# Four interleaved attention layers: VectorE's share of the exponentials chosen tile by tile from its estimated backlog

## The chip, the cores and the metric

The kernel runs on one core of one Trainium2 chip. Five engines work side by side, each on its own in-order queue: TensorE (PE; its weight loads are listed apart as PEld), VectorE (DVE), ScalarE (ACT), GpSimd (POOL) and SyncE (SP), which issues most DMAs. The metric is the device time of one execution in microseconds (us). The kernel before took 2195.17 us, the median of three runs (2189.13 to 2195.78).

## The reference

```
x = A_x                                   # 2048 rows x 640, bf16
x = x + A_ref(layernorm(x), A_wqkv, A_wo) # layer 0: windowed, each row sees the 256 rows up to itself
x = x + B_ref(layernorm(x), B_wqkv, B_wo) # layer 1: full attention
x = x + A_ref(layernorm(x), A_wqkv, A_wo) # layer 2: windowed
x = x + B_ref(layernorm(x), B_wqkv, B_wo) # layer 3: full attention
# each: 32 heads of width 20; q, k, v from x @ wqkv; softmax(q k / sqrt(20)) v; then @ wo
```

A full layer takes the exponential of 32 x 2048 x 2048 scores; these dominate the work.

## The kernel before, in words

Rows are cut into four chunks of 512 (`c`), heads into eight groups of four (`g`). A *unit* is one layer, chunk and head group (`class Unit`). A full unit has 16 key blocks of 128 (`kc`) times 4 heads (`j`): 64 *banks*, a bank being the 128 x 512 scores of one head, one key block and one chunk of queries, one of the eight PSUM banks. Chunk 0 of a full layer is split into parts by key blocks (`PARTS`), so that it can begin before all keys are there.

The program is written out by a planner in Python that runs over *tiles* (`t`, one tick of `state["tick"]` each). In a tile, PE writes up to three banks of scores (L1359) into PSUM banks 0 to 2 (even tiles) or 3 to 5 (odd tiles), and ACT takes their exponential in one instruction (L1387). Some tiles later PE multiplies them by the values (L1420), accumulating in bank 7 (`op`). Between these, `background` gives out work of other kinds as *tasks* (`todo`, ordered by the unit that needs them, and `tails`, which go first): normalisation and its transposes (`t_ln`, L447), projections of values (`t_v`) and of keys and queries (`t_block`), the softmax division (`t_tail`, L1128), the output projection (`t_out`, L579). Every task needs a PSUM bank from `take_m`. After the early part of the program only bank 6 is left for that (`mfree`); its contents are drained by DVE (`evac`, L331) or by the operation of the task. Where a unit needs something that has not been issued, `start_unit` calls `require`, which issues the missing tasks on the spot, ahead of the unit's first scores. `keep_clock` adds matmuls whose result nobody reads (`unread`), so that PE stays active.

Keys, queries and values of the full layers go through DRAM: `t_block` writes keys with a DMA from POOL's queue (L546), and `load_unit` loads them for a unit through SP's queue, values first (L798), then four strips of queries (L810) and keys (L812) by turns. `load_ahead` loads a unit early when everything is ready.

DVE computes some of the exponentials itself. Such banks are *set aside* (`aside`), always in pairs: PE writes the scores of each, DVE turns them into fixed point (L957), and once two are there a chain of four operations on 1024 columns follows (`t_chain`, L969, L978, L980, L982). `side_values` multiplies the result by the values (L1010). The number per unit is fixed ahead: `put_aside` gives 4 to each unit of chunks 1 to 3 of layer 1 (`SIDE_1`), and 6 or 8 by turns to the units of chunks 1 to 3 of layer 3 (`SIDE_3`); the first such unit of layer 3 gets none, the last 4. In layer 1 a set-aside bank takes the third place of a tile, so that ACT gets two banks; the list `tiles` is made in advance and spaces them five tiles apart. In layer 3 (`side["late"]`) the set-aside scores come on top of the tile's three and use bank 6 (`side_scores`, L944).

`state["lag"]` estimates how far DVE is behind, in us: each DVE operation adds its estimated time, each tile takes off the time that ACT needs for it. `side_work` issues operations of a chain while the estimate is below `WORK`; in layer 3, set-aside scores are taken while it is below `LAG`.

The order of the units: layer 0 with chunk 0 of layer 1 woven in; then chunks 1 to 3 of layer 1 with layer 2's finished chunks woven in; then chunk 0 of layer 3 (key blocks 0 to 11, with the last chunk of layer 2 woven in, then key blocks 12 to 15); then chunks 1 to 3 of layer 3.

Of the kernel before, what the change touches and what calls it, by code (L numbers as in the profile page):

```python
# [25 lines left out]
G = 8  # L26
# [13 lines left out]
LAG = 0.5  # L40
WORK = 1.0
SIDE_1 = 4
SIDE_3 = (6, 8)
# [9 lines left out]
def kernel(  # L53
# [272 lines left out]
    def evac(out_, in_):  # L326
        if state["act"]:
            nc.scalar.copy(out=out_, in_=in_)
        else:
            state["lag"] += 0.6  # L330
            nc.vector.tensor_copy(out=out_, in_=in_)  # L331
# [60 lines left out]
    def stats(l, c, i):  # L392
        if (l, c) not in mvs:
            mvs[l, c] = lnp.tile([P, 4, 2], F32, name="mv", tag="mv")
        state["lag"] += 1.2
# [287 lines left out]
    def put_aside(l, c, g):  # L683

        if l == 1:
            n = SIDE_1
        else:
            n = 4 if (c, g) == (NC - 1, G - 1) else SIDE_3[g % 2]
        if n == 2:
            return ((NT - 1, 2), (NT - 1, 3))  # L690
        return tuple((NT - 1 - i // 4, i % 4) for i in range(n))

# [3 lines left out]
    class Unit:  # L696
        def __init__(self, l, c, g, part=None):
            self.l, self.c, self.g, self.part = l, c, g, part
            self.windowed = l % 2 == 0
            self.aside = ()  # L700
            if self.windowed:
                sets = [(m, b0, subs, j) for m, b0, subs in window_banks(c) for j in range(4)]
            else:

                if c > 0 and (l, c, g) != (3, 1, 0):
                    self.aside = put_aside(l, c, g)
                k0, k1 = key_blocks(l, part)
                sets = [
                    (None, 0, [(kc, 0, 4, 0)], j) for kc in range(k0, k1) for j in range(4)
                    if (kc, j) not in self.aside  # L710
                ]
            n = len(sets)
            self.banks = [
                (self, j, m, b0, subs, i < 4, i >= n - 4 + len(self.aside), i == n - 1)
                for i, (m, b0, subs, j) in enumerate(sets)
            ]
# [144 lines left out]
    def finish_unit(u):  # L861
# [31 lines left out]
    side_todo = deque(  # L893
        (u, p, i) for u in units for p in range(len(u.aside) // 2) for i in range(2)
    )
    side_left = Counter({id(u): len(u.aside) for u in units})
    side_out = {}
    side = {"xi": deque(), "chain": deque(), "out": deque(), "late": False}
# [7 lines left out]
    def side_start():  # L906

        assert live["xnT"] == 0 and not side["chain"] 
# [18 lines left out]
    def side_free():  # L927

        if not side_todo or not side["late"]:
            return False  # L930
        u, p, i = side_todo[0]
        return (
            id(u) in loaded and state["tick"] >= loaded[id(u)] + 8
            and mfree[6][0] <= state["tick"] and (i == 1 or len(side["xi"]) > 0)
        )

    def side_scores():

        u, p, i = side_todo[0]
        mseq[0] += 1  # L940
        mfree[6] = (state["tick"] + 2, mseq[0])
        kc, j = u.aside[2 * p + i]
# [4 lines left out]
    def side_fixed(z):  # L947

        u, p, i = side_todo.popleft()
        side_left[id(u)] -= 1  # L950
        if not side_left[id(u)] and id(u) in deferred:
            live["kt"] -= 1
            live["qt"] -= 1
        if i == 0:
            side["now"] = side["xi"].popleft()
        xi = side["now"]
# [33 lines left out]
    def side_work(force):  # L990

        while (force or state["lag"] < WORK) and side["chain"]:
# [11 lines left out]
    def side_values(u, pairs, done):  # L1004

        for n in range(done, len(pairs)):
            pt = pairs[n][0]
            for i in range(2):
                kc, j = u.aside[2 * n + i]
                nc.tensor.matmul(  # L1010
                    op[32 * j : 32 * j + VW, :], lhsT=u.v(kc, j), rhs=pt[:, i, :], start=False,
                    stop=all(jj != j for _, jj in u.aside[2 * n + i + 1 :]),
                    skip_group_check=True,
                )
            side["out"].append(pt)

    def side_push():
# [3 lines left out]
        if side_free():  # L1021
            side_scores()
            return
# [6 lines left out]
    def side_done(u):  # L1030

        n = 0
        while len(side_out.get(id(u), ())) < len(u.aside) // 2:
            n += 1
            assert n < 10000
            side_push()
        return side_out.pop(id(u))
# [5 lines left out]

    def s_emitted(u):
# [6 lines left out]
        elif side_left[id(u)]:  # L1051
# [187 lines left out]
    with tc.manual_schedule():  # L1239
# [11 lines left out]
        banks = [b for u in units for b in u.banks]  # L1251
        tiles = []
        starts = {}
        n = 0
        last_layer = sum(len(u.banks) for u in units[: index[3, 1, 0, None]])
        placed = {}
        while n < last_layer:
            size = 2 if len(tiles) % 2 and narrow(banks[n][0]) else 3
            u = banks[n][0]
            at = placed.setdefault(id(u), [])  # L1260
            extra = []
            if (
                len(at) < len(u.aside) and banks[n + 1][0] is u
                and len(tiles) >= (15 // (SIDE_1 - 1) if SIDE_1 > 2 else 3) * len(at) + (at or [0])[0]
            ):
                kc, j = u.aside[len(at)]
                extra = [(u, j, "side", 0, [(kc, 0, 4, 0)], False, False, False)]
                at.append(len(tiles))
                size = 2
            for b in banks[n : n + size]:  # L1270
                starts.setdefault(id(b[0]), len(tiles))
            tiles.append(banks[n : n + size] + extra)
            n += size
# [249 lines left out]
```

## Time and profile before

| | |
|---|---|
| median of three runs | 2195.17 us (2189.13 to 2195.78) |
| the profiled execution | 2197.81 us |
| its span, first to last instruction | 2196.1 us |
| ACT: exponentials of three banks | 1321, 1816.3 us busy |
| ACT: exponentials of two banks | 245, 261.2 us busy |
| mean granted TensorE clock | 0.993 |

Rows of groups give line, engine, operation, output and inputs with shape, the count, then busy time and mean nanoseconds of one, then the engine's idle time in front of them with what ended it. Rows of waits give who waited for whom, the total in us, the number of waits and the longest. Rows of a timeline give start and length in us, and in brackets the idle time before and its releaser; neighbouring instructions of one kind are merged (x2). Busy time counts overlapping instructions once.

In the profiled execution chunk 1 of layer 1 begins at 497.2 us, chunk 0 of layer 3 at 1284.2, and chunk 1 of layer 3 at 1558.5.

### The profile page before, as it was taken

The page shows a single profiled execution, that of the slowest core. Times are in us where ns is not written, and L with a number is a line of the kernel's source. Part 1 is how long each engine was busy: PE and PEld are TensorE (multiplying, and loading weights), DVE is VectorE, ACT ScalarE, POOL GpSimd, SP SyncE. Part 2 cuts the span into 40 slices and gives each one's busy share as a digit, 9 for nine tenths or more (in the row PEclk, how much of TensorE's full clock was granted, in tenths as well). Part 3 has the DMA queues.
Part 4 walks back from the last instruction along what each step waited for, and adds up shares of the span by engine and source line. Part 5 has one row for each costly group of instructions (what it writes and reads, how often), then busy time and mean ns, then how long its engine had stood idle before and what let it go on. Part 6 is the DMA issues. An engine that isn't in the chain of part 4 may idle for free. (4 is left out here: it accounts for less than half of the span.)

```text
span 2196.1 us, 73000 instructions
## 1 busy us (share of the span) xinstructions
PE 1931.1 (88%) x31782; PEld 760.4 (35%) x31783; DVE 1324.3 (60%) x2308; ACT 2112.9 (96%) x1726; POOL 483.3 (22%) x952
## 2 busy tenths in 40 slices
PE   8999998988889888888888988888888988888887
PEld 3444443433333333333333433342222222222222
DVE  5556565425656666566665743532487778778873
ACT  7789899999999999999999999999999999999997
POOL 6665556110121113401143112511000000000000
PEclk9899999999999999999999999999999999999999
DMA  6223233322210323112231123122112111111100
GB/s 201 74 82 107 68 98 99 81 78 64 74 46 27 83 60 90 39 37 64 64 101 34 35 86 98 39 57 65 48 43 61 32 32 41 35 32 35 53 20 17
DMA packets 88416, 137.27 MB, mean 63 GB/s; under 512 B 20766, under 2 KB 63486, under 8 KB 88094
## 3 DMA queue, kind: packets, MB, share of 16 engines
q1 hardware_dynamic: 68878, 79.43, 13.1%
q0 software_dynamic: 19216, 53.17, 8.2%
q8 instruction: 249, 4.08, 0.8%
q14 instruction: 73, 0.60, 0.1%
HBM read 99.52 MB, written 27.79 MB: 58 GB/s over the span
## 5 line engine op out<-in xcount | busy, mean ns | idle before, releaser
L1387 ACT ACTIVATE pt<-ps 128x1536 bf16<-128x1536 f32 (+2 forms) x1646 | 2072.1, 1438 | 46.1 <-PE ps L1359 36.1
L1359 PE MATMUL ps<-qt,kt 32*128 32x512 bf16 x3938 | 542.4, 384 | 79.3 <-ACT pt L1387 70.2
L307 PE MATMUL ps<-masks,ident 128*32 128x512 bf16 x5676 | 504.6, 387 | 99.4 <-ACT pt L1387 54.8
L1420 PE MATMUL ps<-pt,vt 128*21 128x512 bf16 x3826 | 383.1, 387 | 1.1 <-issue 1.1
L1359 PEld LDWEIGHTS <-kt 32*128 32x128 bf16 x3938 | 161.0, 91 | 482.7 <-issue 461.0
L307 PEld LDWEIGHTS <-ident 128*32 128x32 bf16 x5676 | 179.9, 94 | 283.1 <-issue 254.7
L1463 POOL TENSOR_SCALAR_AFFINE_SELECT pt<-pt 128x256 bf16<-128x256 bf16 (+2 forms) x505 | 213.2, 444 | 184.4 <-ACT pt L1387 181.8
L307 PE MATMUL ps<-xnT,wqk 128*32 128x512 bf16 x3320 | 224.8, 381 | 12.4 <-DVE on L1128 2.8
L331 DVE CAST st<-ps 128x512 bf16<-128x512 f32 x134 | 92.7, 691 | 169.1 <-PE ps L307 164.9
L1420 PEld LDWEIGHTS <-vt 128*21 128x21 bf16 x3842 | 95.0, 89 | 254.9 <-issue 251.5
L957 DVE TENSOR_SCALAR xnT<-ps 128x512 int32<-128x512 f32 x158 | 109.2, 691 | 109.2 <-PE ps L944 108.4
L307 PE MATMUL ps<-wop,on 128*32 128x320 bf16 x3712 | 160.9, 300 | 6.8 <-DVE x_sb L579 3.3
L1474 DVE TENSOR_TENSOR pt<-pt,masks 128x512 bf16<-128x512 bf16 (+4 forms) x267 | 111.3, 433 | 61.3 <-ACT pt L1387 59.8
L307 PEld LDWEIGHTS <-on 128*32 128x32 bf16 x5760 | 122.2, 95 | 66.6 <-issue 33.6
L1359 PE MATMUL ps<-qa,ka 32*128 32x384 bf16 (+2 forms) x1408 | 114.5, 278 | 24.4 <-ACT pt L1387 21.2
L307 PE MATMUL ps<-wv,xnT 128*32 128x320 bf16 x2560 | 116.6, 302 | 7.9 <-DVE on L1128 3.3
L579 DVE TENSOR_TENSOR x_sb<-x_sb,ps 128x320 bf16<-128x320 bf16 x120 | 58.3, 486 | 105.8 <-PE ps L307 104.9
L307 PEld LDWEIGHTS <-wqk 128*32 128x32 bf16 x3320 | 83.5, 96 | 95.9 <-issue 38.0
L1128 DVE TENSOR_TENSOR on<-on,ps 128x512 bf16<-128x512 bf16 x128 | 86.3, 683 | 47.8 <-PE ps L307 46.9
L885 DVE CAST on<-ps 128x512 bf16<-128x512 f32 x112 | 77.1, 688 | 61.7 <-PE ps L1010 36.1
L957 DVE TENSOR_SCALAR raw_o<-ps 128x512 int32<-128x512 f32 x96 | 66.1, 689 | 61.4 <-PE ps L1359 60.3
L546 POOL DMA_DIRECT2D k_d<-st x75 | 42.6, 568 | 224.2 <-DVE st L331 209.1
(101 smaller groups left out, 1638.5 us busy)
## 6 DMA issues: line engine op xcount, KB each, us to landing
vt<-v_d SPq DMA_DIRECT2D x48, 336.0 KB
kt<-k_d SPq DMA_DIRECT2D x192, 80.0 KB
wqk<-in_B_wqkv_dram POOLq DMA_DIRECT2D x80, 160.0 KB, 3.5
wqk<-in_A_wqkv_dram POOLq DMA_DIRECT2D x70, 160.0 KB, 3.5
k_d<-st POOLq DMA_DIRECT2D x75, 128.0 KB, 2.3
q_d<-st POOLq DMA_DIRECT2D x75, 128.0 KB, 2.1
qt<-q_d SPq DMA_DIRECT2D x384, 20.0 KB
v_d<-vs POOLq DMA_DIRECT2D x16, 336.0 KB, 3.1
```

The source lines that it names most:

```text
L307: nc.tensor.matmul(out_[r], lhsT=lhsT[:, r], rhs=rhs, start=start, stop=stop)
L331: nc.vector.tensor_copy(out=out_, in_=in_)
L546: nc.gpsimd.dma_start(out=dst, in_=staging.pop())
L579: nc.vector.tensor_tensor(out=xv, in0=had, in1=yp, op=ALU.add)
L885: nc.vector.tensor_copy(out=oT, in_=op)
L957: nc.vector.tensor_scalar(out=xi.bitcast(I32)[:, i * C : (i + 1) * C], in0=z, scalar1=SCALE * LOG2E * FIX, scalar2=127.5 * FIX, op0=ALU.mu ...
L1128: nc.vector.tensor_tensor(out=oT, in0=oT, in1=zb, op=ALU.mult)
L1359: nc.tensor.matmul(sp[:, i, col * P : (col + qn) * P], lhsT=u.k(kc, j), rhs=u.q(j, q0, qn), start=True, stop=True,)
L1387: nc.scalar.activation(out=pt[:, i:k, b0 * P :], in_=sp[:, i:k, b0 * P :], func=ACT.Exp, scale=SCALE,)
L1420: nc.tensor.matmul(op[32 * j : 32 * j + VW, q0 * P : (q0 + qn) * P], lhsT=u.v(kc, j), rhs=pg[:, i, col * P : (col + qn) * P], start=(first ...
L1463: nc.gpsimd.affine_select(out=v, in_=v, compare_op=ALU.is_gt if later else ALU.is_ge, fill=0.0, base=0, pattern=[[0, k - i], [-1 if later ...
L1474: nc.vector.tensor_tensor(out=pt_[:, i:k, cols], in0=pt_[:, i:k, cols], in1=mv_, op=ALU.mult)
```

## The change

Units keep a deque of the banks still to do (`rest`) instead of a fixed list, and tiles are put together when they are issued (`take`, `next_tile`). `side_giver` picks the unit that gives a pair of banks to DVE: the first of up to three units that is loaded for at least eight ticks, in work with at least 12 banks left, or not begun and with at least `KEEP` (30) left. The pair is taken from the end of the unit's banks (`side_take`). This happens in any tile where the estimated backlog is below `LAG_1` or `LAG`; one pair's second bank follows when the next tile allows it. Counts per unit are no longer fixed, and chunk 0 of layer 3 takes part too: `side_start` comes once the last part of layer 2 is through, from unit 4 of that chunk on, and not at its end. The estimates in `lag` are changed for two kinds of operation, and `rate`, which paces the tasks, counts with the units' sizes in place of the list of tiles. Values of finished pairs are multiplied whenever they are three ticks old.

```diff
 LAG = 0.5
+LAG_1 = 0.5
 WORK = 1.0
-SIDE_1 = 4
-SIDE_3 = (6, 8)
+WORK_1 = 1.0
+KEEP = 30
+MOST_1 = 64
...
-            state["lag"] += 0.6
+            state["lag"] += 0.7 if in_.shape[-1] == C else 0.5
...
-        state["lag"] += 1.2
+        state["lag"] += 1.1
...
+        def pop(self):
+            if self.windowed:
+                return self.rest.popleft()
+            kc, j = self.rest.popleft()
+            end = not self.rest
+            return (self, j, None, 0, [(kc, 0, 4, 0)], kc == self.k0, end, end)
...
+    givers = [u for u in units if not u.windowed and (u.l, u.c) != (1, 0)]
...
-        assert live["xnT"] == 0 and not side["chain"] 
+        assert live["xnT"] <= 2 and not side["chain"] and side["half"] is None
...
+    def side_giver():
+        if side["half"] is not None:
+            return side["half"][0]
+        if not side["xi"]:
+            return None
+        while side["at"] < len(givers) and not givers[side["at"]].rest:
+            side["at"] += 1
+        for n in range(side["at"], min(side["at"] + 3, len(givers))):
+            u = givers[n]
+            if id(u) not in loaded or state["tick"] < loaded[id(u)] + 8:
+                return None
+            if not side["late" if u.l == 3 else "early"]:
+                return None
+            if u.l == 1 and len(u.aside) >= MOST_1:
+                continue
+            if len(u.rest) >= (KEEP if len(u.rest) + len(u.aside) < u.size else 12):
+                side["at"] = n
+                return u
+        return None
+
+    def side_take(u):
+        if side["half"] is not None:
+            return side["half"][1]
+        j = u.rest.pop()
+        i = u.rest.pop()
+        u.aside += (i, j)
+        side["half"] = (u, i, j)
+        return i
...
-        while (force or state["lag"] < WORK) and side["chain"]:
+        while (force or state["lag"] < (WORK if side["late"] else WORK_1)) and side["chain"]:
...
+        def next_tile(t, giver):
+            if state["unit"] < final:
+                size = 2 if t % 2 and narrow(flow[0]) else 3
+                if giver is None or giver.l == 3 or size == 2:
+                    return take(size)
+                kc, j = side_take(giver)
+                return take(2) + [(giver, j, "side", 0, [(kc, 0, 4, 0)], False, False, False)]
             size = 3
-            if side_now:
-                return [banks.popleft() for _ in range(min(size, len(banks)))]
-            if t % 2 and not tails and state["held"] is None and mfree[6][0] < state["tick"]:
-                if all(task.wake > state["tick"] for task in todo) :
+            if giver is None and t % 2 and not tails and state["held"] is None and mfree[6][0] < state["tick"]:
+                if all(task.wake > state["tick"] for task in todo):
                     size = 4
-            return [banks.popleft() for _ in range(min(size, len(banks)))]
+            return take(size)
...
-            if t < len(tiles) or banks:
-                if t >= len(tiles) and not side["late"] and not live["xnT"] and not todo:
+            if flow:
+                if not side["early"] and state["unit"] >= index[1, 1, 0, None]:
+                    side_early()
+                if (
+                    not side["late"] and state["unit"] >= index[3, 0, 4, PARTS[3][0]]
+                    and live["xnT"] <= 1 and not live["qa"] and not live["ka"]
+                ):
                     side_start()
-                side_now = (
-                    state["held"] is None and state["lag"] < LAG and side_free()
-                )
-                cur = next_tile(t)
+                if state["unit"] >= final:
+                    last_tick[0] = 0
+                giver = side_giver() if state["lag"] < (LAG if side["late"] else LAG_1) else None
+                if giver is not None and giver.l == 3 and (
+                    state["held"] is not None or mfree[6][0] > state["tick"]
+                ):
+                    giver = None
+                cur = next_tile(t, giver)
...
+                elif giver is not None and giver.l == 3:
+                    side_scores(giver)
...
-                if first:
-                    valued = 0
-                if u.aside and not end:
-                    pairs = side_out.get(id(u), ())
-                    if len(pairs) > valued and pairs[valued][1] + 3 <= state["tick"]:
-                        if valued + 1 < len(u.aside) // 2:
-                            side_values(u, pairs[: valued + 1], valued)
-                            valued += 1
-                if end and u.aside:
-                    side_values(u, side_done(u), valued)
+                if u.aside:
+                    if end:
+                        side_done(u)
+                    else:
+                        side_values(u, 3)
```

Left out are the bookkeeping of `side_fixed`, `side_done` and `s_emitted`, and the new `rate`, which divides the tasks' remaining work by the units' distance in tiles as before.

## The prediction

> **What bounds the kernel now.** I read the page's busy table first, then busy time by stretch, then who waits for whom inside the stretch that the change touches most. Single instructions came last.
>
> ```profile
> PE 1931.1 (88%) x31782; PEld 760.4 (35%) x31783; DVE 1324.3 (60%) x2308; ACT 2112.9 (96%) x1726; POOL 483.3 (22%) x952
> ...
> 497.20:1284.20 787.00, 687.96 (x11543) 281.94 (x11539) 492.72 (x866) 774.29 (x625) 173.06 (x323) 1.00 0.22 59
> 1284.20:1558.50 274.30, 236.30 (x4006) 97.48 (x4002) 96.15 (x202) 272.95 (x204) 66.47 (x123) 0.99 0.24 67
> 1558.50:2196.10 637.60, 559.58 (x7412) 176.04 (x7405) 466.68 (x621) 621.71 (x460) 0.00 (x0) 0.99 0.12 36
> ```
>
> The last three rows are stretches: chunks 1 to 3 of the second layer with the third layer woven in; chunk 0 of the final layer; the rest. Columns: bounds, length, then busy time of PE, weight loads, DVE, ACT, POOL. ACT is busy 98 to 99% in the first two, so an exponential taken from it is worth its price, as long as PE and DVE still feed it.
>
> **What a bank costs ACT.** Consecutive exponentials overlap, so their price is the distance between starts.
>
> ```profile
> 580.16 2.45 ACT L1387 ACTIVATE pt<-ps 128x1536 bf16<-128x1536 f32 x2
> 581.49 2.46 ACT L1387 ACTIVATE pt<-ps 128x1024 bf16<-128x1024 f32 x2
> 582.40 2.90 ACT L1387 ACTIVATE pt<-ps 128x1536 bf16<-128x1536 f32 x2
> ```
>
> A three-bank tile takes 581.49 - 580.16 = 1.33 us, a two-bank tile 582.40 - 581.49 = 0.91 (others 0.90): 0.427 a bank. Counted from both programs, set-aside banks go from 254 to 350: 96 to 164 in the second layer, 0 to 22 in chunk 0 of the final layer, 158 to 164 after it. ACT has 77 three-bank tiles fewer and 68 two-bank tiles more: -77 x 1.33 + 68 x 0.905 = -40.9, with small shapes **-41.4 us**. By stretch: 68 x 0.427 = -29.0; 22 x 0.427 = -9.4; 6 x 0.427 = -2.6, and -0.4 for fewer instructions.
>
> **What it costs DVE and PE in the first stretch.**
>
> ```profile
> L957 DVE TENSOR_SCALAR raw_o<-ps 128x512 int32<-128x512 f32 x96 | 66.1, 689 | 61.4 <-PE ps L1359 60.3
> L980 DVE SCALAR_TENSOR_TENSOR raw_o<-raw_o 128x1024 f16<-128x1024 f16 x48 | 58.5, 1220 | 0.9
> ...
> PE ps L1359 <- ACT pt L1387: 45.2, 148, 0.6
> PE ps L307 <- DVE st L331: 9.5, 22, 1.0
> PE ps L307 <- DVE on L1128: 8.4, 19, 0.9
> PE ps L307 <- ACT pt L1387: 8.1, 28, 0.7
> ```
>
> A pair costs DVE 2 x 0.69 (L957) + 0.69 (L969) + 0.69 (L978) + 1.22 (L980) + 1.22 (L982) = 5.2 us; the three lines not shown have rows of the same kind. 34 more pairs are 177 us on 493, in a stretch that is to shrink to 758: 88% busy where it was 63%. PE's work stays. It waits 53 us there for ACT (45.2 + 8.1) and some 32 for DVE, seven rows like the two shown. So PE is busy or held by DVE for 734 of 787 us, and has 53 us to give before it binds in ACT's place. The cost of too little room shows already:
>
> ```profile
> 567.54 0.68 DVE L957 TENSOR_SCALAR raw_o<-ps 128x512 int32<-128x512 f32 x1
> 568.14 0.68 DVE L1128 TENSOR_TENSOR on<-on,ps 128x512 bf16<-128x512 bf16 x1
> 568.87 0.40 PE L307 MATMUL ps<-masks,ident 128*32 128x512 bf16 x4 [0.92 <-DVE on L1128]
> 569.92 1.45 ACT L1387 ACTIVATE pt<-ps 128x1536 bf16<-128x1536 f32 x1 [0.48 <-PE ps L1359]
> ```
>
> The set-aside bank's read (L957) stands ahead of a scaling (L1128) on DVE. PE waits for the scaling to free bank 6, and the next scores stand behind that wait: ACT idles 0.48. Start to start over all 608 tiles, the 96 tiles with a set-aside bank and the 96 behind them lose 20.8 us over the distances above, 0.22 for each such bank; the other 416 tiles lose 8, or 0.02 each. So a bank worth 0.427 gives back about 0.19 net of that background: 13 us for 68. The old plan spaced its banks five tiles apart or more; in the new one 38 of 163 distances are one tile and 36 two, beside a DVE a quarter fuller. I take 0.32 a bank, 22 us: **-29 + 22 = -7**. Bounds: nothing lost, -29; 0.65 a bank, +15.
>
> **What it costs in chunk 0 of the final layer.** The 22 banks go through bank 6, the only bank left there for projections and tails, and each holds it for two tiles. In the changed program's order the output projection of the third layer's last chunk ends 28 tiles later, at tile 1109 (before: 1081). Tile 1111 opens the first unit that needs that chunk's keys and values, while its normalisation, values and first key block have not been issued. `require` then issues them all ahead of the tile's scores: 276 matmuls in a row, where the old order had at most about one such step between two tiles here. The steps alternate PE and DVE on one bank:
>
> ```profile
> 1455.69 0.39 PE L307 MATMUL ps<-masks,ident 128*32 128x512 bf16 x4
> 1456.42 0.49 DVE L331 COPY xnT<-ps 128x640 bf16<-128x640 bf16 x1 [0.94 <-PE ps L447]
> ...
> 1462.55 0.86 PE L307 MATMUL ps<-wv,xnT 128*32 128x320 bf16 x20
> 1463.46 0.49 DVE L331 CAST vs<-ps 128x320 bf16<-128x320 f32 x1 [0.96 <-PE ps L307]
> ...
> 1476.93 0.69 DVE L331 CAST st<-ps 128x512 bf16<-128x512 f32 x1 [2.54 <-PE ps L307]
> 1477.93 0.56 POOL L546 DMA_DIRECT2D k_d<-st  x1 [0.50 <-DVE st L331]
> 1480.72 0.28 SPq L812 DMA_DIRECT2D kt<-k_d  x1
> ...
> 1556.50 2.03 DMA kt<-k_d
> ```
>
> Four normalised blocks at 0.73 + 0.49 + 0.06 = 1.28: 5.1. Eight value groups at 0.91 + 0.49 + 0.05 = 1.45: 11.6. One key group: 1.25 (L307, twenty matmuls on wqk) + 0.06 + 0.69 + 0.06 = 2.1. Then the keys go through DRAM: cast ended 1477.62, first load issued 1480.72 (3.1 later, SP's queue held until the write lands), third strip 1.45 later (three issue pairs in SP's queue), landing 2.03, scores and semaphores 0.4: 7.0. With 0.7 for the first normalised rows that is 26.5. PE scores a tile once ACT is done with the tile before last, and has spent about 1.0 on scores, values and a dummy group when it enters, so ACT still holds 2 x 1.33 - 1.0 = 1.7 of work: **ACT stands for about 25 us**; bounds 18 (DMA faster, more ahead) and 32. Behind it the remaining key blocks come in lumps: the next unit's second block has 6 tiles (8.0) for a path of about 9.7, 1.7 late. The output projection comes in eight lumps of 1.1 us, each within one tile; with 0.4 of scores and 0.3 to 0.4 of values they exceed the tile by about 0.45: 3.6. Together **+5.3**, bounds 0 and 8. The transfers before and after are the same ones, only later.
>
> The Trainium skill, "TensorE: Matmul & The Clock Gate" (Part 1, the clock gate), says the array drops to half clock after an idle window of about 3.4 us. Some 7 us of the stall are a bare DMA wait, so by that page the first 3.4 us behind it would run slow, at most 3 us more, and the sum would be 14; the stretches above have no such gap, and their granted clock is 0.99 to 1.00.
>
> **After it** -3, bounds -4 and +2: DVE is at 73% there already and ACT at 98%, and only 6 banks come. The first 497 us keep their instruction counts; only background order shifts: 0, bounds 3 either way.
>
> **The sum.** -7 - 9.4 + 25 + 5.3 - 3 = **+11 us**. The profiled execution took 2197.8 (span 2196.1): 2209. It stands 2.6 above the median of the runs, 2195.2; from that median, **2206**.
>
> **Rivals.**
> - Layer two loses nothing more (faster). For it: 53 us of PE waiting on ACT, and half of the set-aside tiles show a clean 0.90. Against it: DVE at 88%, adjacent set-aside tiles. It decides from a loss of 0.06 a bank downwards, where the sum passes -6.6. With none: -29 - 9.4 + 25 + 5.3 - 3 = -11: 2184.
> - DVE becomes the bound of layer two. For it: 88% busy in one in-order queue, where the drains that free bank 6 stand behind operations of 1.22 us. Against it: the planner issues these only below one microsecond of estimated backlog. 0.65 a bank: +15 in place of -7, +33 in all: 2228.
> - The catch-up costs half, 12 us, because PE and DVE of neighbouring steps overlap or ACT has more in store. For it: only that the estimate is a chain of eleven terms. Against it: one bank, strict alternation. -2: 2193.
>
> That fewer banks move than it says is excluded by the counts.
>
> **How the numbers follow.** Forecast 0.48, rivals 0.17, 0.15, 0.20. A measurement tells 0.3%, 6.6 us, from no change. The forecast's own range is 2195 to 2216; a fifth to a third of it lies within 0.3%. Faster: the first rival, less its edge, and a little of the third, 0.16. Same: most of the third and 0.11 of the forecast, 0.30. Slower: the rest, 0.54. Range 2181 to 2227, between the first two rivals, leaves out a tenth on each side.
>
> **What would show it.** One ACT gap of 18 to 32 us, near 1480, released by PE L1359, with a chain of copies and casts (L331) and then a load of keys before it. In layer two DVE near 88% and PE's waits for DVE about 55 us. ACT's busy time down by some 45. Wrong if that gap is below 12, or if layer two shrinks by more than 20 us or grows.

## The result, and the profile after

The changed kernel takes 2246.3 us, the median of four runs (2238.55 to 2251.24). The kernel before took 2192.98 on the same chip. The ratio is 1.0241, with a 95% interval of 1.0206 to 1.0276: slower by 2.4%, where 0.5% had been forecast. The profiled execution took 2251.2 (span 2249.4), 53.3 us more of span than before.

First the busy table of the page, then busy time in the same three stretches as before (bounds, length, PE, weight loads, DVE, ACT, POOL, granted clock, which is the share of its full clock that PE got, DMA share, GB/s). Line numbers have moved: L1359 is now L1381, L1387 is L1405, L957 is L976, L331 is L333, and L307 is L309.

```profile
PE 1968.9 (88%) x31914; PEld 759.9 (34%) x31915; DVE 1556.8 (69%) x2599; ACT 2083.1 (93%) x1716; POOL 501.3 (22%) x957
...
494.70:1312.70 818.00, 713.04 (x11557) 280.21 (x11554) 658.02 (x1074) 755.12 (x626) 189.47 (x328) 0.98 0.21 57
1312.70:1617.70 305.00, 257.59 (x4126) 101.75 (x4122) 149.90 (x269) 265.89 (x198) 67.75 (x123) 0.95 0.22 60
1617.70:2249.40 631.70, 554.76 (x7402) 174.10 (x7402) 479.95 (x639) 617.35 (x457) 0.00 (x0) 1.00 0.13 36
```

Two stretches lost and none gained much:

| stretch | before | after | change | forecast |
|---|---|---|---|---|
| up to chunk 1 of layer 1 | 497.2 | 494.7 | -2.5 | 0 |
| layers 1 and 2 | 787.0 | 818.0 | +31.0 | -7 |
| chunk 0 of the final layer | 274.3 | 305.0 | +30.7 | +21 |
| the rest | 637.6 | 631.7 | -5.9 | -3 |

ACT was busy 98% of layers 1 and 2 before. Now it is 755.12 / 818.00 = 92%, and 87% in chunk 0. So the exponentials did leave ACT, and ACT waited for longer than it had saved.

The waits inside the stretch of layers 1 and 2 (who waited for whom, total, times, longest) show on whom:

```profile
ACT pt L1405 <- PE ps L1381: 53.4, 89, 2.6
PE ps L1381 <- ACT pt L1405: 23.4, 75, 0.6
...
PE ps L309 <- DVE st L333: 15.5, 29, 1.4
...
PE ps L309 <- DVE on L1151: 12.4, 20, 1.5
...
PE ps L309 <- ACT pt L1405: 6.0, 15, 0.7
```

PE's waits for ACT fell from 53 us to 29 (23.4 + 6.0). Its waits for DVE, the two rows shown and the smaller ones like them, rose from 32 to 63. ACT's idle time behind PE's scores rose from 11.0 to 53.4. No engine is full (ACT is at 92%, PE at 87%, DVE at 80%); the three take turns waiting.

One place in the timeline shows how. Rows give start, length, engine, line, operation, and in brackets the idle time before and its releaser:

```profile
568.03 1.22 DVE L999 SCALAR_TENSOR_TENSOR raw_o<-raw_o 128x1024 f16<-128x1024 f16 x1
...
569.09 0.59 PE L309 MATMUL ps<-wv,xnT 128*32 128x320 bf16 x12
569.28 1.23 DVE L1001 SCALAR_TENSOR_TENSOR raw_o<-raw_o 128x1024 uint16<-128x1024 int32 x1
...
570.64 0.69 DVE L976 TENSOR_SCALAR raw_o<-ps 128x512 int32<-128x512 f32 x1
571.25 0.48 DVE L333 CAST va<-ps 128x320 bf16<-128x320 f32 x1
...
571.79 0.62 PE L309 MATMUL ps<-xnT,wqk 128*32 128x512 bf16 x4 [1.46 <-DVE va L333]
572.34 1.03 PE L1381 MATMUL ps<-qt,kt 32*128 32x512 bf16 x3
573.04 1.02 ACT L1405 ACTIVATE pt<-ps 128x1024 bf16<-128x1024 f32 x1 [1.48 <-PE ps L1381]
...
576.68 2.88 ACT L1405 ACTIVATE pt<-ps 128x1536 bf16<-128x1536 f32 x2 [2.61 <-PE ps L1381]
```

A value projection is complete at 569.68 (569.09 + 0.59). The cast that empties bank 6 starts only at 571.25, because two operations for set-aside banks (L1001, L976) stand ahead of it in DVE's queue. PE wants bank 6 for its next projection and stands 1.46 us; the scores are queued behind that projection, so ACT stands 1.48. Then the projections and scores run slowly, and ACT stands 2.61 more. The granted clock goes with the second part, in the next row against a row of undisturbed work:

```profile
571.50:581.70 10.20, 9.65 (x73) 2.37 (x72) 4.21 (x7) 4.78 (x5) 2.71 (x4) 0.50 0.16 45
634.00:654.00 20.00, 18.73 (x275) 6.32 (x267) 18.37 (x27) 19.40 (x17) 0.00 (x0) 1.00 0.01 2
```

For 10.2 us PE ran at half clock, and ACT was busy 4.78 of them. In the whole stretch PE spent 37.5 us at half clock, in nine places; before, 3.4 us in one.

The forecast's one large gap is there too, in chunk 0. These rows are the burst that `require` issues ahead of tile 1111:

```profile
1527.14 0.72 PE L449 MATMUL ps<-ident,xn 128*32 128x128 bf16 x20 [2.93 <-DVE xn L429]
...
1533.68 1.53 PE L309 MATMUL ps<-wv,xnT 128*32 128x320 bf16 x20 [0.59 <-DVE xnT L333]
...
1535.26 0.49 DVE L333 CAST vs<-ps 128x320 bf16<-128x320 f32 x1 [1.63 <-PE ps L309]
1535.80 1.53 PE L309 MATMUL ps<-wv,xnT 128*32 128x320 bf16 x20 [0.59 <-DVE vs L333]
...
1548.46 0.86 PE L309 MATMUL ps<-wv,xnT 128*32 128x320 bf16 x20 [0.60 <-DVE vs L333]
...
1556.26 1.06 PE L1381 MATMUL ps<-qt,kt 32*128 32x512 bf16 x2 [5.08 <-DMA kt<-k_d]
...
1558.31 2.79 ACT L1405 ACTIVATE pt<-ps 128x1536 bf16<-128x1536 f32 x2 [32.95 <-PE ps L1381]
```

ACT stands 32.95 us. The chain is the predicted one, PE and DVE by turns on one bank and then the keys through DRAM. But a value step lasts 1535.80 - 1533.68 = 2.12 us and not 1.45, because its twenty matmuls take 1.53 and not 0.86; the last, at 1548.46, is back at 0.86. PE's granted clock was 0.50 from 1527.2 to 1547.7 and again for 6.8 us from 1554.5.

### The profile page after: what moved, and what is told of

Its sections match the earlier page's. It is cut to its first block, busy times and chain, and to the rows that moved or that the text cites. A ratio compares the mean times of both kernels' runs of the same rounds, so it can differ in the third digit from the quotient of the medians.

```text
span 2249.4 us, 73554 instructions
## 1 busy us (share of the span) xinstructions
PE 1968.9 (88%) x31914; PEld 759.9 (34%) x31915; DVE 1556.8 (69%) x2599; ACT 2083.1 (93%) x1716; POOL 501.3 (22%) x957
## 5 line engine op out<-in xcount | busy, mean ns | idle before, releaser
L1405 ACT ACTIVATE pt<-ps 128x1536 bf16<-128x1536 f32 (+2 forms) x1636 | 2042.0, 1378 | 131.1 <-PE ps L1381 113.0
L309 PE MATMUL ps<-masks,ident 128*32 128x512 bf16 x5808 | 515.9, 387 | 119.0 <-ACT pt L1405 56.5
L1381 PE MATMUL ps<-qt,kt 32*128 32x512 bf16 x3910 | 553.3, 386 | 50.2 <-ACT pt L1405 38.7
L1381 PEld LDWEIGHTS <-kt 32*128 32x128 bf16 x3910 | 148.4, 91 | 458.9 <-issue 432.9
L309 PEld LDWEIGHTS <-ident 128*32 128x32 bf16 x5808 | 182.1, 94 | 314.2 <-issue 290.5
L1476 POOL TENSOR_SCALAR_AFFINE_SELECT pt<-pt 128x384 bf16<-128x384 bf16 (+2 forms) x510 | 229.1, 473 | 195.5 <-ACT pt L1405 184.5
L309 PE MATMUL ps<-xnT,wqk 128*32 128x512 bf16 x3320 | 231.6, 387 | 17.7 <-DVE st L333 4.2
L976 DVE TENSOR_SCALAR xnT<-ps 128x512 int32<-128x512 f32 x186 | 128.5, 691 | 130.3 <-PE ps L960 129.2
L333 DVE CAST st<-ps 128x512 bf16<-128x512 f32 x134 | 92.5, 691 | 137.7 <-PE ps L309 137.1
L309 PE MATMUL ps<-wop,on 128*32 128x320 bf16 x3712 | 160.8, 300 | 6.1 <-DVE x_sb L581 3.1
L309 PEld LDWEIGHTS <-on 128*32 128x32 bf16 x5760 | 123.9, 96 | 64.4 <-issue 32.5
L1487 DVE TENSOR_TENSOR pt<-pt,masks 128x512 bf16<-128x512 bf16 (+4 forms) x270 | 117.7, 452 | 31.5 <-ACT pt L1405 30.1
L309 PE MATMUL ps<-wv,xnT 128*32 128x320 bf16 x2560 | 121.7, 311 | 18.2 <-DVE vs L333 7.9
L1381 PE MATMUL ps<-qa,ka 32*128 32x384 bf16 (+2 forms) x1408 | 118.6, 279 | 19.8 <-ACT pt L1405 16.0
L976 DVE TENSOR_SCALAR raw_o<-ps 128x512 int32<-128x512 f32 x164 | 112.4, 687 | 21.2 <-PE ps L1381 13.4
L309 PEld LDWEIGHTS <-wqk 128*32 128x32 bf16 x3320 | 86.7, 97 | 105.8 <-issue 49.2
L1151 DVE TENSOR_TENSOR on<-on,ps 128x512 bf16<-128x512 bf16 x128 | 86.2, 683 | 37.6 <-PE ps L309 36.8
L1001 DVE SCALAR_TENSOR_TENSOR raw_o<-raw_o 128x1024 uint16<-128x1024 int32 x82 | 100.8, 1229 | 1.3
L999 DVE SCALAR_TENSOR_TENSOR raw_o<-raw_o 128x1024 f16<-128x1024 f16 x82 | 100.5, 1226 | 1.4
```

The costliest lines, as they stand in the source:

```text
L309: nc.tensor.matmul(out_[r], lhsT=lhsT[:, r], rhs=rhs, start=start, stop=stop)
L976: nc.vector.tensor_scalar(out=xi.bitcast(I32)[:, i * C : (i + 1) * C], in0=z, scalar1=SCALE * LOG2E * FIX, scalar2=127.5 * FIX, op0=ALU.mu ...
L999: V.scalar_tensor_tensor(out=q, in0=q, scalar=TB, in1=t, op0=ALU.add, op1=ALU.mult)
L1001: V.scalar_tensor_tensor(out=po.bitcast(U16), in0=xi.bitcast(I32), scalar=1.0 / C, in1=q, op0=ALU.mult, op1=ALU.add,)
L1151: nc.vector.tensor_tensor(out=oT, in0=oT, in1=zb, op=ALU.mult)
L1381: nc.tensor.matmul(sp[:, i, col * P : (col + qn) * P], lhsT=u.k(kc, j), rhs=u.q(j, q0, qn), start=True, stop=True,)
```

## The experiments

All ratios are against the kernel before, run on the same chip. Lengths are of each profiled execution, in us. "Banks" counts the set-aside banks of layer 1, and "half" the time at half clock of the falls that begin in the stretch of layers 1 and 2 (in e2, e5 and e12 the last one runs on up to 7 us past its end).

| run | banks | ratio (95%) | layers 1, 2 | half | chunk 0 | rest |
|---|---|---|---|---|---|---|
| before | 96 | 1 | 787.0 | 3.4 | 274.3 | 637.6 |
| the change | 164 | 1.0241 (1.0206 to 1.0276) | 818.0 | 37.5 | 305.0 | 631.7 |
| e1, chunk 0 gives no bank | 164 | 1.0119 (1.0100 to 1.0139) | 817.6 | 37.5 | 272.8 | 634.2 |
| e2, old number in layer 1 | 96 | 1.0242 (1.0226 to 1.0259) | 814.9 | 23.9 | 306.7 | 631.1 |
| e3, filler as for three banks | 164 | 1.0265 (1.0243 to 1.0287) | 816.8 | 27.3 | 304.9 | 631.7 |
| e4, thin chains | 164 | one execution, 2204.7 us | 768.1 | 0 | 306.0 | 631.7 |
| e5, old number, spaced | 96 | 1.0164 (1.0145 to 1.0184) | 794.3 | 10.2 | 305.9 | 631.2 |
| e6, spaced, no limit | 112 | 1.0120 (1.0104 to 1.0136) | 786.6 | 10.2 | 302.5 | 631.5 |
| e7, smaller backlog | 132 | 1.0131 (1.0105 to 1.0156) | 789.0 | 0 | 303.6 | 631.3 |
| e8, tasks before banks | 164 | 1.0150 (1.0133 to 1.0166) | 819.2 | 41.0 | 279.2 | 631.6 |
| e9, spaced, chunk 0 gives none | 112 | 0.9984 (0.9971 to 0.9997) | 785.2 | 6.8 | 272.8 | 634.6 |
| e11, e9 with free heads only | 98 | 0.9994 (0.9981 to 1.0007) | 790.3 | 3.4 | 272.9 | 633.9 |
| e12, old number, thin chains | 96 | one execution, 2236.9 us | 803.8 | 10.2 | 306.7 | 631.2 |
| e13, burst filled | 164 | 1.0224 (1.0206 to 1.0242) | 811.3 | 20.5 | 299.4 | 631.6 |

**e1: is the burst due to chunk 0 giving banks?**

```diff
-    givers = [u for u in units if not u.windowed and (u.l, u.c) != (1, 0)]
+    givers = [u for u in units if not u.windowed and u.c > 0]
```

> The changed kernel, but chunk 0 of the final layer gives no banks to VectorE. Theory (the set-aside scores hold bank 6 and push the last chunk's projections into the catch-up at tile 1111): no gap there, the stretch of chunk 0 takes 274 us as before instead of 305, the whole about 30 us less than the changed kernel, ratio to before about 1.010. Rival (the gap comes from the new pacing of the tasks or from the changed backlog estimates): the gap stays and the stretch takes about 300.

The gap at tile 1111 is gone, chunk 0 is at 272.8, and the time falls by 29 us. So half of the loss is shown to come from that part of the change; layers 1 and 2 are untouched by it.

**e2: is it the number of banks in layer 1?**

```diff
-MOST_1 = 64
+MOST_1 = 4
```

> The changed kernel, but each unit of layer 1 gives at most 4 banks as before (96 instead of 164). Theory (the number of banks given in layer 1 costs the time there): layers 1 and 2 take about 787 us instead of 818, the clock hardly drops, ratio to before about 1.010. Rival (the new planner, its tile by tile choice or its pacing, costs the time whatever the number): the stretch stays above 805.

The theory fell. With the old plan's 96 banks the stretch is still 814.9. Its last tile takes 9.1 us, 7.8 too many: another burst of `require`, a value group, a key group and the keys through DRAM, in front of chunk 0 of the final layer. Why that work is late there was not tried. Without this gap the stretch is still 20 above the old plan. The banks are now bunched: as soon as the backlog estimate allows it, the next pair is taken, so a unit's four come early and close together.

**e3: do the added matmuls of `keep_clock` matter?** A tile that gives a bank away counts as two banks there.

```diff
+                n_pe = n_b
                 if cur[-1][2] == "side":
...
-                background(t, n_b)
+                background(t, n_pe)
```

> The changed kernel, but a tile with a set-aside bank gets the quota of unread matmuls of a three-bank tile. Theory (VectorE's queue delays the drains of bank 6; clock drops follow from PE's waits): no help, layers 1 and 2 take 818 us within 6, clock still drops. Rival (the quota cut for two-bank tiles lets the clock drop, and the drops cost 15 us or more): no more than two drops, the stretch takes 803 or less.

816.8 in place of 818.0, and the clock still falls (27.3 us at half clock): the rival fell.

**e4: is it DVE's queue?** The four operations of a chain run on 64 of 1024 columns in layer 1, so DVE has the same instructions in the same order with little work in them; the rest of the output tile is filled once at the start.

```diff
+        w = 64 if u.l == 1 else 2 * C
+        t = t[:, 0:w]
...
-        po = pt.rearrange("p a b -> p (a b)")
+        po = pt.rearrange("p a b -> p (a b)")[:, 0:w]
```

> The changed kernel, but in layer 1 the four chain operations work on 64 of 1024 columns, so most exponentials of set-aside banks are left out; matmuls, scores, the read of the scores and the order stay the same. Theory (VectorE's queue is the cause): layers 1 and 2 take 770 us or less, PE waits for VectorE under 25 us, no more than two clock drops. Rival (tiles with two banks for ScalarE are too short for PE, whatever VectorE does): the stretch stays above 800.

The stretch's row, then PE's two waits for DVE that were shown above (L1151 is L1154 here):

```profile
497.00:1265.00 768.00, 691.74 (x11556) 279.83 (x11554) 418.70 (x1075) 748.43 (x626) 172.58 (x328) 1.00 0.23 61
```

```profile
PE ps L309 <- DVE st L333: 8.7, 21, 0.5
PE ps L309 <- DVE on L1154: 7.3, 17, 0.9
```

With the same instructions DVE is busy 418.7 us and not 658.0. PE's waits for DVE halve (27.7 in all, a little above what was expected), the longest of these two from 1.5 to 0.9, and PE never falls to half clock. The stretch is 50 us shorter. So 50 us pass through the length of DVE's chains, the half clock included. They do not all belong to what the set-aside banks cost more than before (60 us, worked out further down): the chains of as many banks as before had are thin here too, and DVE has less work than the 492.72 us of before.

**e5: is it the bunching?** The old number, and five tiles from one bank to the next. The planner's threshold for units in work rises with it, since four spaced banks need more tiles.

```diff
-MOST_1 = 64
+MOST_1 = 4
+SPACE = 5
...
-            if len(u.rest) >= (KEEP if len(u.rest) + len(u.aside) < u.size else 12):
+            if len(u.rest) >= (KEEP if len(u.rest) + len(u.aside) < u.size else 12 if u.l == 3 else 26):
...
+                if giver is not None and giver.l == 1:
+                    if t < side["next"]:
+                        giver = None
+                    else:
+                        side["next"] = t + SPACE
```

> The changed kernel with at most 4 banks per unit of layer 1, as in the run with four per unit, but set-aside banks at least five tiles apart as in the kernel before. Theory (bunched banks cost the time in that run: VectorE gets a pair's 5.2 us within a few tiles): layers 1 and 2 up to chunk 0 of the final layer take 792 us or less, where that run took 806 without its last gap, and the loss in tiles with a set-aside bank and behind them falls to about 0.22 a bank. Rival (the new pacing of the tasks or the changed estimates): 802 us or more. The first unit of the final layer and tile 1111 still force their catch-ups.

The rows of e2 and of e5 for the stretch, in this order:

```profile
491.10:1306.00 814.90, 704.43 (x11806) 286.52 (x11805) 488.52 (x864) 777.43 (x624) 171.37 (x318) 0.99 0.21 55
```

```profile
492.20:1286.50 794.30, 692.33 (x11686) 282.19 (x11685) 489.59 (x865) 774.55 (x627) 172.36 (x319) 1.00 0.21 57
```

DVE does the same work in both (488.5 and 489.6), and the spaced one is 20.6 us shorter; both contain the burst at the end. Without it (9.5 us for that tile, 8.2 too many) e5 is at 786, and the old plan at 787. The theory holds: at this number of banks and apart from that burst, all that the tile-by-tile choice lost is the spacing. One sum does not show it: PE's waits for DVE are 31.5 us in e2 and 31.4 in e5. What grew is ACT's idle time behind PE's scores, which makes 28 us in e2 without the last gap and 9.5 in e5; e12 comes back to this.

**e6 and e7: how many banks pay when they are spaced, or taken at a smaller backlog?** e6 is e5 without `MOST_1`. e7 has the change's own rule with lower limits:

```diff
-LAG_1 = 0.5
+LAG_1 = 0.1
...
-WORK_1 = 1.0
+WORK_1 = 0.6
```

> The changed kernel with set-aside banks of layer 1 at least five tiles apart and no other limit: 112 banks. Theory (spacing is what counts): 112 banks take 6.8 us from ScalarE against the 96 of before and lose 0.22 each, so layers 1 and 2 take 783 to 790 us. Rival (VectorE's total load counts, not the spacing): with 8 pairs more than before still close to before, 787 to 795, and the run with four per unit and spacing equals the one without.

> The changed kernel with tighter limits on the estimated backlog in layer 1 (banks taken below 0.1 in place of 0.5, chain operations below 0.6 in place of 1.0): 132 banks. Theory (the drains of bank 6 are late behind VectorE's chains): the waits of PE for VectorE fall below 45 us and layers 1 and 2 take 790 to 800 us. Rival (bunching alone, whatever the limits): the loss per bank stays near 0.5 and the stretch takes 808 or more.

112 spaced banks give 786.6, in the theory's range and 0.4 below the rival's, whose other condition, that e5 equals e2, fell. 132 sparingly chosen ones give 789.0, a little below the theory's range, and PE's waits for DVE are 33.5 us; the rival of e7 fell. The stretch took 787.0 with 96. So the banks past the old number gave back in losses what they took from ACT, in each way that was tried.

**e8: can chunk 0 give banks and let the tasks go first?**

```diff
                     and live["xnT"] <= 1 and not live["qa"] and not live["ka"]
+                    or state["unit"] < final and (tails or any(k.wake <= state["tick"] for k in todo))
```

> The changed kernel, but in chunk 0 of the final layer a bank is given only where no task or tail is ready to run, so bank 6 goes to them first: 4 banks there in place of 22. Theory (the set-aside scores kept bank 6 from the tasks): no gap at tile 1111, the stretch of chunk 0 takes 271 to 276 us, the whole some 30 us less than the changed kernel. Rival (the gap comes from the pacing or from VectorE's load in that stretch): the gap stays above 15 us.

The gap at tile 1111 is gone with four banks left in chunk 0, so it was the banks taken ahead of the tasks that put these off. The median is 23 us below the changed kernel's, where some 30 had been expected. The chunk is at 279.2, 3 above what was expected, for a reason of its own:

```profile
1475.78 0.60 PE L1031 MATMUL ps<-ka,vt 128*21 128x512 bf16 x2 [4.76 <-DVE ka L1001]
...
1477.46 1.45 ACT L1406 ACTIVATE pt<-ps 128x1536 bf16<-128x1536 f32 x1 [5.21 <-PE ps L1382]
```

The unit ended before the chain of its pair had run. Its last values need the pair, so PE stands through the whole chain (4.76 us), and ACT 5.21.

**e9 and e11: what is left when both losses are taken out?** e9 is e6 and e1 together. e11 adds that a bank waits for a tile whose other two banks belong to other heads.

```diff
+                    row = side["half"][1][1] if side["half"] else giver.rest[-2][1]
+                    near = [b[1] for w in list(flow)[:2] for b in list(w.rest)[:2]][:2]
-                    if t < side["next"]:
+                    if t < side["next"] or row in near:
```

> The changed kernel with both repairs: set-aside banks of layer 1 at least five tiles apart, and none from chunk 0 of the final layer. Theory (the two places found are all that the change lost): stretches of about 786, 273 and 633 us after a first of 476, together 10 to 16 us less than the kernel before's span, ratio 0.993 to 0.998. Rival (the catch-up or the bunching only hid another loss): ratio above 1.003.

> The run with both repairs, and a set-aside bank waits for a tile whose two other banks use other heads of the group, so that its scores need not queue for the same rows of the array: 98 banks in place of 112. Theory (part of the loss per bank is that queueing): the loss per bank falls from about 0.16 to 0.1, layers 1 and 2 take 780 to 786 us in spite of 14 banks less. Rival (rows do not matter, spacing and VectorE's queue do): 788 to 792 us, as 14 banks go back to ScalarE.

The row of e9 for the stretch:

```profile
491.40:1276.60 785.20, 689.90 (x11567) 281.40 (x11563) 533.73 (x916) 769.64 (x627) 181.32 (x325) 1.00 0.22 60
```

e9 took 2188.84 us against 2190.48 for the kernel before, with 12 and 23 runs. It is the only version whose interval lies below the kernel before, by 0.16%. The stretches came out as expected (785.2, 272.8 and 634.6); the ratio did not, as the expectation counted from the profiled execution of before, 2197.81, which lies 7.3 us above that median. The gain is so little that I would not build on it: the 16 added banks took 6.8 us from ACT's work (16 x 0.427), and the stretch is 1.8 shorter. e11 shows no gain; its 790.3 us are what the rival expected, for which the heads of a tile's other banks do not matter.

**e12: is bunching harmful through DVE alone?** e2 with e4's thin chains.

> The run with four banks per unit, bunched, and the four chain operations of layer 1 on 64 of 1024 columns, so that most of those exponentials are left out. Theory (bunched banks cost time through VectorE's queue): layers 1 and 2 before the last gap take 786 us or less in place of 806. Rival (adjacent two-bank tiles cost it by themselves): 800 or more.

Before its last gap, which is as long as in e2 (9.1 us), the stretch takes 794.7 us, between the two expectations. Of the 20.6 us between e2 and e5, 814.9 - 803.8 = 11.1 go with the length of the chains and 9.5 stay. They stay where tiles in a row give a bank: one that comes right behind another loses 0.40 us on average, in e2 and here alike, and a lone one 0.21 in e2 and 0.17 here. So bunching has a cost that does not come from the length of DVE's chains. These rows, with the columns as above, hold two such tiles in a row:

```profile
714.70:715.91 1.21, 1.21 (x16) 0.42 (x15) 0.79 (x2) 1.21 (x3) 0.00 (x0) 1.00 0.00 0
715.91:717.54 1.63, 1.63 (x36) 0.85 (x36) 1.09 (x2) 1.02 (x3) 0.00 (x0) 1.00 0.04 10
```

```profile
715.95 1.13 PE L309 MATMUL ps<-wop,on 128*32 128x320 bf16 x28
...
717.01 0.39 PE L1384 MATMUL ps<-qt,kt 32*128 32x512 bf16 x3
...
717.54 3.71 ACT L1408 ACTIVATE pt<-ps 128x1536 bf16<-128x1536 f32 x3 [0.61 <-PE ps L1384]
```

PE is busy all the time, with a lump of the output projection ahead of the scores, and ACT, through with its two banks after 1.02 us, waits 0.61 for them. A tile that gives a bank away takes ACT 0.905 us instead of 1.33, but PE still has its three banks of scores and its share of the tasks to do. In e12, 32 of these tiles come right behind another. In the 20 of them that lose over 0.2 us, PE is busy 94% of the time, counted from the start of the tile before to that of the next. That is e4's rival at a smaller size; no run with less work on PE tested it.

**e13: why was the gap 33 us and not 25?** PE gets groups of four matmuls, which nobody reads, in the pauses of the burst.

```diff
+            fill = state.get("fill")
             if t is None:
                 state["tick"] += 1
+                for _ in range(6 if fill is not None and n < 8 else 0):
+                    by_columns(ps[:, fill, :], ident, masks[:, 0, :], True, True)
                 continue
+            freed = mseq[0]
             state["credit"] = max(state["credit"] - advance(t), -1.0)
+            if fill is not None and mseq[0] > freed:
+                by_columns(ps[:, fill, :], ident, masks[:, 0, :], True, True)
...
+                        state["fill"] = 3 * (t % 2) if (u.l, u.c) == (3, 0) else None
                         start_unit(u)
+                        state["fill"] = None
```

> In the burst at tile 1111, and nowhere else, PE gets groups of four matmuls that nobody reads, written to a scores bank that stands empty: six groups (2.4 us) while the first normalised rows are awaited, and one (0.39 us) behind each of the 13 steps that free bank 6, inside the 0.6 us in which PE waits for DVE there. Theory (the half clock, set off by the thin work of PE in the burst, is the term that made the gap 33 us and not 25): the granted clock stays at 1.00 from the first transposes to the key group, a value step goes from 2.12 to 1.45 us and a normalised block from 1.74 to 1.28, the gap of ACT from 33.0 to 25 to 27, chunk 0 from 305 to 297 to 300, the ratio from 1.024 to about 1.021. The half clock behind the wait for the keys stays. Rival (the clock falls whatever fills these pauses, because of a state of the chip that the burst only coincides with): clock 0.50 for some 20 us again, steps of 2.1 us, gap 32 to 34. Third (the added groups lengthen the steps): clock 1.00, steps of 1.8 or more, gap over 30.

The same steps in its timeline, then the clock over them:

```profile
1526.10 0.86 PE L315 MATMUL ps<-wv,xnT 128*32 128x320 bf16 x20 [0.38 <-DVE xnT L339]
1526.78 0.40 PE L315 MATMUL ps<-masks,ident 128*32 128x512 bf16 x4
1527.01 0.49 DVE L339 CAST vs<-ps 128x320 bf16<-128x320 f32 x1 [0.96 <-PE ps L315]
1527.56 0.86 PE L315 MATMUL ps<-wv,xnT 128*32 128x320 bf16 x20 [0.38 <-DVE vs L339]
...
1545.89 2.79 ACT L1413 ACTIVATE pt<-ps 128x1536 bf16<-128x1536 f32 x2 [26.43 <-PE ps L1389]
```

```profile
1518.00:1538.00 20.00, 14.01 (x340) 8.25 (x339) 8.90 (x18) 1.45 (x2) 5.01 (x7) 1.00 0.28 57
```

A value step takes 1527.56 - 1526.10 = 1.46 us, the clock stays at 1.00, and the gap is 26.4. More work on PE made the burst shorter by 6.5 us. The theory holds, and the other two fall. In the time of the whole kernel this does not stand out of the noise (1.0224 against 1.0241, with overlapping intervals).

## Why the prediction missed

**Direction right, size wrong.** 2206 had been forecast, in 2181 to 2227; 2246.3 came. One of the two things named as proof against it, that layer two grows, happened; the gap of 18 to 32 us came as 33. Against the sum of +11 the span grew by 53.3. The difference of 42.3 is layers 1 and 2 (38), the gap (8), the lumps (1.7), the rest (-2.9) and the beginning (-2.5).

**What a bank saves ACT: right.** By the same distances between starts, ACT's work in layers 1 and 2 went from 758.2 to 729.2 us, the -29.0 of the prediction.

**The step that failed: "I take 0.32 a bank, 22 us".** By those distances, the losses in that stretch rose from 28.7 to 88.8. That is 60 us for 68 banks, 0.88 each: twice what a bank saves, and past the upper bound of 0.65. The step took the average loss of banks that stood five tiles apart, and raised it by half for being closer. But the loss of a bank depends on what stands beside it: on DVE's queue, as the thin chains of e4 and e12 show, and, in a tile that follows another such tile, on PE's own work. e5 gave the old loss at the old number when spaced, and e2 some 20 us more with that number bunched. The rest comes with the number: 164 banks, as closely bunched, lose another 40 (88.8, against 48.8 in e2 without its last gap). The prediction had the right place in hand, the scaling behind a set-aside read at 568 us, but averaged such places into a price for each bank, where it was the first link of a queue.

**"PE has 53 us to give before it binds in ACT's place" is the other half of that error.** (The 734 us in front of it are 787 - 53; busy time and waits for DVE make 720, the other 14 are short waits of other kinds.) PE's waits for DVE came out near the forecast (63 for 55), and PE still waited 29 us for ACT. The two waits don't draw on one account: PE waits for DVE in one tile and ACT runs dry, and in another tile PE waits for ACT. In e12's rows PE binds within a single tile, while over that whole stretch it waits 68 us for ACT. DVE's work was as counted (+165 us for +177); its share is 80% and not 88%, because the stretch grew.

**The rival "DVE becomes the bound of layer two" had the mechanism and not its size.** It named the drains of bank 6 behind operations of 1.22 us, and the timeline above is just that. It put 0.65 a bank on it. What speaks against it in the prediction, that the planner issues only below one microsecond of estimated backlog, is no protection: two operations of 1.23 and 0.69 us, the first of them just begun, suffice.

**A part that the prediction lacked: the clock.** In four executions with the same plan in layers 1 and 2 (the change, e1, e8, e13) the half-clock time is 37.5, 37.5, 41.0 and 20.5 us and the stretch 818.0, 817.6, 819.2 and 811.3. From the first three (mean 38.7 and 818.3) to the last that is 7.0 us for 18.2, or 0.38 each. By that estimate, which rests on a single difference, the 34 us that the change has more than before (37.5 - 3.4) cost about 13 of the 60.

**The burst: mechanism, place and chain right, one condition wrong.** It came at tile 1111, with the chain as written; "near 1480" became 1525 because the stretch before it grew. Of the 8 us between 25 and 33:

- the eight value groups took 16.2 us (11.6 predicted) and the four normalised blocks 6.5 (5.1), both through the clock;
- the first normalised rows came 2.9 us after PE had run out of work (0.7 predicted), since two POOL operations of 1.04 each on the variance stand ahead of them; that term was left out;
- ACT had 1.15 us in store and not 1.7; the keys' way took 6.4 and not 7.0.

In e13, with the clock held, the value groups took 11.7, the normalised blocks 4.9, and the gap was 26.4. So some 6 of the 8 (4.6 and 1.7) are shown to be the clock.

**The Trainium skill's rule on the clock** ("TensorE: Matmul & The Clock Gate", Part 1), that the array drops to half after an idle window of about 3.4 us, had been applied to one place: the bare wait for the keys. There the trace agrees: the clock falls to 0.50 for 6.8 us, 3.3 us into the wait of 5.08 us (in e13 just behind the wait of 4.70). But the costly drop was elsewhere, at 1527.2, after waits of at most 2.93 us, with PE busy 0.47 of the 3.40 us before. It lasted 20.5 us, through steps in which PE was busy 1.53 of 2.12. In layers 1 and 2 no wait of PE is longer than 1.9 us, and the clock fell in nine places. The measurement decides: a thinly filled window can be enough. How thin, no run shows: in the same stretch PE was busy 2.39 of the 3.43 us before the fall at 1155.1, and 1.96 of 3.40 us from 1288.3 on without a fall.

**The smaller terms.** Lumps and the late second block cost 30.7 + 9.4 - 33.1 = 7.0 (5.3 predicted; 33.1 is the gap by distance between starts). The rest of the final layer gained 5.9 (3 predicted, outside its bound of 4). ACT's busy time fell by 30 and not 45: in the rows above an exponential that starts alone shows 1.45 us, while one that overlaps the next takes up 1.33.

## What to carry to other kernels

An average loss per unit of side work, read from a plan that spaces it, is no price for a plan that bunches it: look at what stands ahead in the in-order queue of the engine that also empties the shared buffer, and at what the engine that feeds both still has to do in the shortened step. A choice by estimated backlog that sees only the engine giving the work away, and not the buffer or the tasks put off, is paid for twice: at once, and later in one burst. Where two engines alternate on one buffer, time the chain at the clock that it will have, since thin work can lower it, and work that nobody reads can make the chain faster.

## What the runs showed of the hardware

- PE's granted clock fell to 0.50 where the 3.4 us before were 36 to 70% busy (the nine places in layers 1 and 2), without any wait over 1.9 us. The busy share alone does not tell a fall: 58% went by at full clock. It stayed down for multiples of about 3.4 us: 3.4, 6.8, 10.2 and 20.5.
- In one execution the falls begin a whole number of 3.413 us apart: in the change's at 571.45, 731.88 (47 steps on) and 745.53 (4 more). The same plan of layers 1 and 2 spent 20.5 to 41.0 us at half clock in four executions.
- At half clock the same steps keep PE busier (14.57 of 20.50 us in the burst, 71%), and still it took 20.5 us for the clock to come back, with nothing changed in the steps. What ended it no run shows.
